# A fused attention and MLP block: a reciprocal root handed out in four pieces, weight loads moved behind transposes, the first V groups reordered, the last output columns narrowed

## The chip, the cores and the metric

The kernel runs on one core of one Trainium2 chip. The metric is the device time of one execution in microseconds (us), lower is better.

Terms: in the lines of the profile PE is the matmuls of TensorE, PEld its weight loads, DVE is VectorE, ACT ScalarE, POOL GpSimd, SPq the queue of SyncE; names such as r_a are buffers of the program. The granted clock is TensorE's clock as a share of its full speed. A drain is an instruction, here of DVE or ACT, that reads a finished accumulator, so that TensorE can use it again. A turn is a transpose. The root is the reciprocal root in a normalization.

## The reference

One transformer block in bf16: a pre-norm sliding-window attention with residual, then a pre-norm MLP with SiLU and residual. 2048 tokens, width 1024, 32 heads of 32, a window of 256 keys, hidden width 3584.

```python
x = A_x                                                     # [1, 2048, 1024]
h = x + A(_layernorm(x), A_wqkv, A_wo)                      # window attention, 32 heads x 32, W = 256
h2 = h + silu(_layernorm(h) @ B_w1) @ B_w2                  # 1024 -> 3584 -> 1024
return h2
```

## The kernel before

The tokens go in four blocks of 512. TensorE (matmul engine) is kept busy by interleaving: projections of block b with attention of block b-1, the output projection with attention of the last block, and at the end a dense stage without attention. In the dense stage each block has 28 groups of the first product (`h1_group`, 8 matmuls each) and then 8 output groups of the second product (28 matmuls each). Small work of other engines is kept in lists of steps, and the loops hand out one or two after each group.

The normalization of one block for the MLP (called LN2 here; LN1 is that before the attention) is such a list: a load of `h`, four statistics, one reciprocal root (12 tiny DVE operations), four normalizations, and four transposes by DMA. (The code here is cut at `...`, and some comments are added.)

```python
    def ln2_steps(b):
        ...
        steps = [load]
        steps += [lambda j=j: ln_stats(hb[:, j, :], st, j) for j in range(4)]
        steps.append(lambda: ln_rstd(st, rs, 0, 4))
        for j in range(4):
            steps.append(lambda j=j: ln_norm(hb[:, j, :], st, rs, j))
        turns = [lambda j=j: ln_transpose(hb[:, j, :], ln2T[b], j) for j in range(4)]
        return steps[:-2] + [turns[0], steps[-2], turns[1], steps[-1]] + turns[2:]
```

In the dense stage the LN2 steps of the *next* block are handed out, two after each of the eight output groups; what is left is issued after the last one. The next block's first product reads all four transposes (`rhs=ln2T[b][:, kt, :]` covers all 512 tokens).

```python
    for b in range(NB):
        ...
        for ft in range(FT):                       # 28 groups of the first product
            acc = h1_group(b, ft)
            run_late()                             # issues the transposes of attention
            if extra:                              # b == 0: rest of the last attention group
                extra.pop(0)[0]()
                if not extra and b == 0:
                    for i in (1, 2, 3, 4):
                        load_w2(i)                 # 1 MB each
            ...
        steps = ln2_steps(b + 1) if b + 1 < NB else []
        ...
        for j in range(4):
            ...
            for c in range(2):                     # 8 output groups
                ...                                # 28 matmuls, a DVE add, a store on the queue
                for _ in range(2):
                    if steps:
                        steps.pop(0)()
        while steps:
            steps.pop(0)()
```

All loads, stores and DMA transposes are issued from one queue (SyncE, "SPq" in the lines of the profile). The first V groups at the start of the kernel and the output projection (`wo_group`, which hands out LN2 of block 0 from its step n = 9 on) are in the whole kernel:

The softmax here doesn't subtract the row's maximum and nothing guards it: scores larger than these inputs give would overflow.

## Time and profile before

| | before |
|---|---|
| time, median of 3 runs | 709.64 us (708.79 to 709.89) |
| span of the profiled run, from first to last instruction | 708.9 us |
| TensorE busy | 695.2 us, 98% |
| longest waits of TensorE | 5.3, 1.6, 1.5 (in two), 1.3 us |
| first Q group starts (the V groups of the start end there) | 25.73 us |
| first dense matmul to first matmul of the second product (block 0) | 295.93 to 367.14 us |

The profiled run took 710.91 us, somewhat more than the median. TensorE is the bound; read its waits and the chain of waits, not the busy shares of the others. The lines are in the prediction.

### The profile page before, as it was taken

The page shows a single profiled execution, that of the slowest core. Times are in us where ns is not written, and L with a number is a line of the kernel's source. Part 1 is how long each engine was busy: PE and PEld are TensorE (multiplying, and loading weights), DVE is VectorE, ACT ScalarE, POOL GpSimd, SP SyncE. Part 2 cuts the span into 40 slices and gives each one's busy share as a digit, 9 for nine tenths or more (in the row PEclk, how much of TensorE's full clock was granted, in tenths as well). Part 3 has the DMA queues.
Part 4 walks back from the last instruction along what each step waited for, and adds up shares of the span by engine and source line. Part 5 has one row for each costly group of instructions (what it writes and reads, how often), then busy time and mean ns, then how long its engine had stood idle before and what let it go on. Part 6 is the DMA issues. An engine that isn't in the chain of part 4 may idle for free.

```text
span 708.9 us, 12138 instructions
## 1 busy us (share of the span) xinstructions
PE 695.2 (98%) x5006; PEld 332.8 (47%) x5006; DVE 288.0 (41%) x606; ACT 259.7 (37%) x335; POOL 172.9 (24%) x375
## 2 busy tenths in 40 slices
PE   8999999999999999979999999999999999999998
PEld 3444555555555554534444444444444444444443
DVE  5347645834443448523332423325134352243111
ACT  3416667777777777511220013300033200233000
POOL 1006566777777777500000000000000000000000
PEclk9999999999999999989999999999999999999999
DMA  9540322125011899780122320021410032200110
GB/s 301 173 120 8 46 54 75 32 55 180 16 23 18 279 265 333 201 276 31 45 69 90 80 75 1 0 67 59 78 35 0 1 97 67 75 1 0 31 38 22
DMA packets 75127, 60.55 MB, mean 85 GB/s; under 512 B 48960, under 2 KB 59200, under 8 KB 75072
## 3 DMA queue, kind: packets, MB, share of 16 engines
q1 hardware_dynamic: 75072, 59.78, 29.9%
q8 instruction: 39, 0.64, 0.4%
q14 instruction: 16, 0.13, 0.1%
HBM read 39.85 MB, written 8.39 MB: 68 GB/s over the span
## 4 chain that ended last, share of the span: by engine, by line
PE 94%; DMA 4%; DVE 2%; SPq 0%; issue 0%
PE hacc L446 18%; PE hacc L483 17%; PE acc L220 16%; PE acc L483 10%; PE acc L446 9%; PE acc L212 8%; PE acc L239 5%; PE o_ps L293 5%; PE sc L257 4%; DMA r_a<-r_n 2%; DMA r_w<-in_A_wqkv_dram 1%; PE hacc L239 1%; DMA r_a<-in_A_x_dram 1%; DVE ln_st L157 0%; DVE r_t L241 0%
## 5 line engine op out<-in xcount | busy, mean ns | idle before, releaser
L268 ACT ACTIVATE r_e<-sc 128x1024 bf16<-128x1024 f32 (+2 forms) x192 | 175.8, 967 | 67.5 <-PE sc L257 54.5
L283 POOL TENSOR_SCALAR_AFFINE_SELECT r_e<-r_e 128x256 bf16<-128x256 bf16 (+1 forms) x368 | 169.9, 490 | 123.1 <-ACT r_e L268 119.7
L446 PEld LDWEIGHTS <-r_w 128*128 128x128 bf16 x896 | 87.8, 98 | 106.1 <-issue 2.4
L483 PEld LDWEIGHTS <-r_a 128*128 128x128 bf16 x896 | 87.7, 98 | 105.7
L483 PE MATMUL hacc<-r_a 128*128 128x512 bf16 x560 | 122.3, 379 | 0.0
L446 PE MATMUL hacc<-r_e,r_w 128*128 128x512 bf16 x456 | 100.9, 379 | 0.0
L455 ACT ACTIVATE r_n<-hacc 128x512 f32<-128x512 f32 x30 | 17.9, 597 | 178.9 <-PE hacc L446 178.9
L483 PE MATMUL acc<-r_a 128*128 128x512 bf16 x336 | 74.0, 379 | 0.0
L220 PEld LDWEIGHTS <-r_w 128*128 128x128 bf16 x512 | 46.1, 98 | 58.6 <-issue 8.9
L222 DVE CAST r_a<-acc 128x512 bf16<-128x512 f32 x56 | 38.6, 690 | 81.0 <-PE acc L220 55.8
L293 PEld LDWEIGHTS <-r_e 128*128 128x128 bf16 x1440 | 50.3, 96 | 22.7
L220 PE MATMUL acc<-r_t,r_w 128*128 128x512 bf16 x256 | 60.8, 380 | 0.0
L220 PE MATMUL acc<-r_w 128*128 128x512 bf16 x256 | 58.2, 380 | 0.0
L293 PE MATMUL o_ps<-r_a,r_e 128*128 128x33 bf16 x1440 | 51.2, 178 | 0.0
L239 PE MATMUL acc<-r_o,r_a 128*128 128x512 bf16 x208 | 49.4, 380 | 1.3 <-DVE r_t L241 1.3
L446 PE MATMUL acc<-r_e,r_w 128*128 128x512 bf16 x216 | 49.1, 379 | 0.0
L239 PEld LDWEIGHTS <-r_a 128*128 128x128 bf16 x256 | 23.3, 98 | 37.2 <-issue 7.4
L257 PE MATMUL sc<-r_a 32*128 32x128 bf16 (+2 forms) x704 | 37.2, 276 | 0.0
L496 DVE SCALAR_TENSOR_TENSOR r_t<-hacc,r_t 128x512 bf16<-128x512 f32 x20 | 13.7, 683 | 56.3 <-PE hacc L483 56.2
L446 PE MATMUL hacc<-r_a,r_w 128*128 128x512 bf16 x144 | 34.6, 393 | 0.0
L496 DVE SCALAR_TENSOR_TENSOR r_t<-acc,r_t 128x512 bf16<-128x512 f32 x12 | 8.3, 692 | 64.2 <-PE acc L483 64.2
L456 DVE SCALAR_TENSOR_TENSOR r_a<-r_n,hacc 128x512 bf16<-128x512 f32 x30 | 20.6, 688 | 33.1 <-ACT r_n L455 33.1
(65 smaller groups left out, 425.4 us busy)
## 6 DMA issues: line engine op xcount, KB each, us to landing
r_w<-in_B_w_dram SPq DMA_DIRECT2D x8, 896.0 KB, 6.8
r_a<-in_B_w_dram SPq DMA_DIRECT2D x7, 1024.0 KB, 9.0
r_w<-in_A_wqkv_dram SPq DMA_DIRECT2D x5, 1024.0 KB, 11.8
r_o<-in_A_x_dram SPq DMA_DIRECT2D x16, 256.0 KB, 5.0
h_dram<-r_t SPq DMA_DIRECT2D x16, 256.0 KB, 2.9
r_t<-h_dram SPq DMA_DIRECT2D x16, 256.0 KB, 2.8
out_dram<-r_t SPq DMA_DIRECT2D x32, 128.0 KB, 1.7
r_e<-h_dram SPq DMA_DIRECT2D x3, 1024.0 KB, 5.8
```

What stands on the lines that cost most here:

```text
L212: nc.tensor.matmul(acc, lhsT=lnT_b[b % 2][:, kt, j * P:(j + 1) * P], rhs=wqkv[:, kt, col0:col0 + 512], start=(kt == 0), stop=(kt == KT - 1))
L220: nc.tensor.matmul(acc, lhsT=wqkv[:, kt, col0:col0 + P], rhs=lnT_b[b % 2][:, kt, :], start=(kt == 0), stop=(kt == KT - 1))
L222: copy(out=(qT, kT)[which][b][:, g, :], in_=acc)
L239: nc.tensor.matmul(acc, lhsT=qT[b][:, g, j * P:(j + 1) * P], rhs=wo[:, g, c * 512:(c + 1) * 512], start=(g == 0), stop=(g == G - 1))
L257: nc.tensor.matmul(sc[hh // 2][:, hh % 2, ch * P:(ch + nq) * P], lhsT=kT[t // 4][r0:r0 + DH, g, (t % 4) * P:(t % 4 + 1) * P], rhs=qT[b][r0 ...
L268: nc.scalar.activation(out=e[:, :, lo:hi], in_=sc[pair][:, :, lo:hi], func=ACT.Exp, scale=scale)
L283: nc.gpsimd.affine_select(out=ap, in_=ap, pattern=[[0, 2], [0, n], [sgn, P]], compare_op=ALU.is_ge if upper else ALU.is_gt, fill=0.0, base ...
L293: nc.tensor.matmul(o_ps[pair][:, qt * 2 + hh, 0:VW], lhsT=e_of(i, kind, pair)[:, hh, ch * P:(ch + 1) * P], rhs=v[:, b * 4 + kt, g * 4 + pa ...
L446: nc.tensor.matmul(acc, lhsT=w1[:, kt, ft * P:(ft + 1) * P], rhs=ln2T[b][:, kt, :], start=(kt == 0), stop=(kt == KT - 1))
L456: nc.vector.scalar_tensor_tensor(out=gT[:, ft, :], in0=th, scalar=1.0, in1=acc, op0=ALU.add, op1=ALU.mult)
L483: nc.tensor.matmul(acc, lhsT=gT[:, ft, j * P:(j + 1) * P], rhs=w2[ft // 4][:, ft % 4, c * 512:(c + 1) * 512], start=(ft == 0), stop=(ft == ...
L496: nc.vector.scalar_tensor_tensor(out=t_out[j % 2][:, c * 512:(c + 1) * 512], in0=acc, scalar=0.5, in1=t_in[j % 2][:, c * 512:(c + 1) * 512 ...
```

## The change

It has four intents: fill the waits for V weights at the start by another order of the V groups; keep DVE from standing in front of TensorE while it computes the root (the root becomes four steps: guess, and three Newton steps); let the last attention transposes go ahead of the w2 loads in the queue; and shorten the tail by narrow last output groups. The diff, cut to its core:

```diff
-    load_wqkv(2 * D, 0, 4)
+    load_wqkv(2 * D)
     load_x(0, 1)
-    load_wqkv(2 * D, 4, 8)
     load_wqkv(2 * D + 512)
...
-    for i in range(14):                              # warm-up matmuls
+    for i in range(11):
...
-    def ln_rstd(st, rs, lo, hi):
+    def rstd_steps(st, rs):
...                                                   # the same 12 operations
+        return [guess, newton, newton, newton]
...                                                   # V groups: (0,0) (0,1) (1,0) (1,1) ...
+    v_group(0, 0, 0, act)                            # now:      (0,0) (1,0) (0,1) (1,1) ...
+    turn_first(x_ring[1], lnT_b[0], 1)
+    ln_first(x_ring[2], st, rs, 2)
+    v_group(0, 1, 0, act)
+    v_group(0, 0, 1, act)
...
-        steps.append(lambda: ln_rstd(st, rs, 0, 4))  # in LN1 and in LN2 of every block
+        steps += rstd_steps(st, rs)
...
-            if n == 9:                               # output projection: LN2 of block 0
+            if n == 8:
                 steps = ln2_steps(0)
                 steps.pop(0)()
-            for _ in range(1 if n < 17 else 2):
-                if steps and n >= 12:
+            for _ in range(1 if n < 18 else 2):
+                if steps and n >= 10:
                     steps.pop(0)()
...
-                if not extra and b == 0:
-                    for i in (1, 2, 3, 4):
-                        load_w2(i)
+            if b == 0 and ft == 3:
+                for i in (1, 2, 3, 4):
+                    load_w2(i)
...
+            if b == NB - 1 and j == 3:
+                cols = [(0, 512), (512, 768), (768, 896), (896, 1024)]
```

More of the change, by code (lines that the diff above doesn't have):

```diff
@@ L126, in load_x, with load_wqkv @@
         nc.sync.dma_start(out=x_ring[(b % 2) * 4 + j], in_=x2d[(b * 4 + j) * P:(b * 4 + j + 1) * P, :])
-    def load_wqkv(c0, k0=0, k1=KT):
-        nc.sync.dma_start(out=wqkv[:, k0:k1, c0:c0 + 512], in_=wqkv_v[:, k0:k1, c0:c0 + 512])
+    def load_wqkv(c0):
+        nc.sync.dma_start(out=wqkv[:, :, c0:c0 + 512], in_=wqkv_v[:, :, c0:c0 + 512])
     load_x(0, 0)
-    load_wqkv(2 * D, 0, 4)
+    load_wqkv(2 * D)
     load_x(0, 1)
-    load_wqkv(2 * D, 4, 8)
     load_wqkv(2 * D + 512)
@@ L158, in ln_stats, with guess, newton @@
         nc.vector.bn_aggr(out=st[:, j, :], in_=stats[:])
-    def ln_rstd(st, rs, lo, hi):
-        n = hi - lo
+    def rstd_steps(st, rs):
         var = small.tile([P, 4], F32, name="ln_var", tag="ln_var")
         t = small.tile([P, 4], F32, name="ln_t", tag="ln_t")
-        va, ta, y = var[:, 0:n], t[:, 0:n], rs[:, lo:hi]
-        nc.vector.tensor_scalar(out=va, in0=st[:, lo:hi, 1], scalar1=LN_EPS, scalar2=None, op0=ALU.add)
-        nc.vector.tensor_scalar(out=y.bitcast(I32), in0=va.bitcast(I32), scalar1=1, scalar2=None, op0=ALU.logical_shift_right)
-        nc.vector.tensor_scalar(out=y.bitcast(I32), in0=y.bitcast(I32), scalar1=-1, scalar2=0x5F3759DF, op0=ALU.mult, op1=ALU.add)
-        for _ in range(3):
+        va, ta, y = var[:], t[:], rs[:]
+        def guess():
+            nc.vector.tensor_scalar(out=va, in0=st[:, :, 1], scalar1=LN_EPS, scalar2=None, op0=ALU.add)
+            nc.vector.tensor_scalar(out=y.bitcast(I32), in0=va.bitcast(I32), scalar1=1, scalar2=None, op0=ALU.logical_shift_right)
+            nc.vector.tensor_scalar(out=y.bitcast(I32), in0=y.bitcast(I32), scalar1=-1, scalar2=0x5F3759DF, op0=ALU.mult, op1=ALU.add)
+        def newton():
             nc.vector.scalar_tensor_tensor(out=ta, in0=y, scalar=-0.5, in1=va, op0=ALU.mult, op1=ALU.mult)
@@ L327 @@
     turn_first(x_ring[0], lnT_b[0], 0)
-    for j in range(4):
-        if j < 3:
-            ln_first(x_ring[j + 1], st, rs, j + 1)
-        v_group(0, j, 0, act)
-        if j < 3:
-            turn_first(x_ring[j + 1], lnT_b[0], j + 1)
-        v_group(0, j, 1, act)
-        if j == 2:
-            dummy = small.tile([P, 1], F32, name="dummy", tag="dummy")
-            nc.scalar.activation(out=dummy[:], in_=eps[:], func=ACT.Exp)
+    ln_first(x_ring[1], st, rs, 1)
+    v_group(0, 0, 0, act)
[3 more added lines that the diff above has]
+    v_group(0, 0, 1, act)
+    turn_first(x_ring[2], lnT_b[0], 2)
+    ln_first(x_ring[3], st, rs, 3)
+    v_group(0, 1, 1, act)
+    v_group(0, 2, 0, act)
+    turn_first(x_ring[3], lnT_b[0], 3)
+    v_group(0, 2, 1, act)
+    dummy = small.tile([P, 1], F32, name="dummy", tag="dummy")
+    nc.scalar.activation(out=dummy[:], in_=eps[:], func=ACT.Exp)
+    v_group(0, 3, 0, act)
+    v_group(0, 3, 1, act)
     for j in range(4):
@@ L355, in ln2_steps @@
         steps += [lambda j=j: ln_stats(hb[:, j, :], st, j) for j in range(4)]
-        steps.append(lambda: ln_rstd(st, rs, 0, 4))
+        steps += rstd_steps(st, rs)
         for j in range(4):
@@ L480, with mm2 @@
         steps = ln2_steps(b + 1) if b + 1 < NB else []
-        def mm2(acc, j, c, first, last):
+        def mm2(acc, j, c0, c1, first, last):
             for ft in range(first, last):
-                nc.tensor.matmul(acc, lhsT=gT[:, ft, j * P:(j + 1) * P], rhs=w2[ft // 4][:, ft % 4, c * 512:(c + 1) * 512],
+                nc.tensor.matmul(acc[:, 0:c1 - c0], lhsT=gT[:, ft, j * P:(j + 1) * P], rhs=w2[ft // 4][:, ft % 4, c0:c1],
                                  start=(ft == 0), stop=(ft == FT - 1))
@@ L488 @@
                 load_h(b, j + 1)
-            accs = [next_acc(), next_acc()]
-            if b == 0 and j == 0:
-                for c in range(2):
-                    mm2(accs[c], j, c, 0, FT - 4)
-            for c in range(2):
-                acc = accs[c]
-                mm2(acc, j, c, FT - 4 if b == 0 and j == 0 else 0, FT)
-                nc.vector.scalar_tensor_tensor(out=t_out[j % 2][:, c * 512:(c + 1) * 512], in0=acc, scalar=0.5,
-                                               in1=t_in[j % 2][:, c * 512:(c + 1) * 512], op0=ALU.mult, op1=ALU.add)
-                nc.sync.dma_start(out=out2d[(b * 4 + j) * P:(b * 4 + j + 1) * P, c * 512:(c + 1) * 512],
-                                  in_=t_out[j % 2][:, c * 512:(c + 1) * 512])
+            cols = [(0, 512), (512, 1024)]
+            if b == NB - 1 and j == 3:
+                cols = [(0, 512), (512, 768), (768, 896), (896, 1024)]
+            accs = [next_acc() for _ in cols]
+            early = FT - 4 if b == 0 and j == 0 else 0
+            for acc, (c0, c1) in zip(accs, cols):
+                mm2(acc, j, c0, c1, 0, early)
+            for acc, (c0, c1) in zip(accs, cols):
+                mm2(acc, j, c0, c1, early, FT)
+                nc.vector.scalar_tensor_tensor(out=t_out[j % 2][:, c0:c1], in0=acc[:, 0:c1 - c0], scalar=0.5,
+                                               in1=t_in[j % 2][:, c0:c1], op0=ALU.mult, op1=ALU.add)
+                nc.sync.dma_start(out=out2d[(b * 4 + j) * P:(b * 4 + j + 1) * P, c0:c1], in_=t_out[j % 2][:, c0:c1])
                 for _ in range(2):
```

## The prediction

> **What bounds the kernel now.** I read the page first, then the waits of TensorE, the chain that ended last, and the order of time on each engine around every gap of TensorE and around the places that the diff touches. TensorE is the bound: it is busy 98% of the span, and the chain runs through it from 12.46 us on. So a part of the change is worth what it does to TensorE's few gaps, and harms only if it makes a new one. The page's busy line, then the waits of TensorE (us in total, times, longest):
>
> ```profile
> PE 695.2 (98%) x5006; PEld 332.8 (47%) x5006; DVE 288.0 (41%) x606; ACT 259.7 (37%) x335; POOL 172.9 (24%) x375
> ...
> PE hacc L239 <- DMA r_a<-r_n: 5.3, 1, 5.3
> PE sc L151 <- DVE r_e L146: 1.6, 1, 1.6
> PE acc L212 <- DMA r_w<-in_A_wqkv_dram: 1.5, 2, 1.2
> PE acc L239 <- DVE r_t L241: 1.3, 1, 1.3
> ```
>
> The longest is one wait for a transpose by DMA of the last attention block (line 313, r_n to r_a). The chain of waits shows it with what follows (start us, us, what):
>
> ```profile
> 303.51 12.64 DMA r_a<-r_n
> 316.16 0.05 issue
> 316.20 0.61 PE hacc L239
> 316.81 3.41 PE hacc L446 x8
> 320.23 2.02 PE hacc L239 x8
> 322.25 1.73 PE hacc L446 x8
> ```
>
> The transpose took 12.64 us where the page has 2.5 us as its median: five w2 loads of 1 MB were issued from 297.98 us on, ahead of it in the same queue, and the DMA engines moved some 390 GB/s until 313. After the gap eight matmuls took 3.41 us where the same group later takes 1.73: the granted clock by single microseconds falls to 0.50 at 313.9 us and comes back at 320.7.
>
> The third place is the change of block in the dense stage, where the kernel before has no gap. In order of time (start us, us, engine, line, operation):
>
> ```profile
> 506.89 0.33 SPq L498 DMA_DIRECT2D out_dram<-r_t  x1
> 507.27 2.61 SPq L178 DMA_TRANSPOSE r_e<-r_e  x2
> 512.02 5.34 PE L446 MATMUL hacc<-r_e,r_w 128*128 128x512 bf16 x24
> 512.22 0.69 DVE L496 SCALAR_TENSOR_TENSOR r_t<-hacc,r_t 128x512 bf16<-128x512 f32 x1 [5.35 <-PE hacc L483]
> 512.94 0.33 SPq L498 DMA_DIRECT2D out_dram<-r_t  x1
> 513.31 0.93 SPq L225 DMA_DIRECT2D r_t<-h_dram  x2
> ```
>
> The last two transposes of the normalized block (line 178) are issued at 507.27, one output group ahead of the end of the block. The next block's first matmul (line 446), which reads all four, starts at 512.02 with no wait. The traffic in the windows of 1 us dies at 511.1, so the margin is under 1 us.
>
> **What the Trainium skill says.** "TensorE: Matmul & The Clock Gate", Part 1 (the HAM clock gate): the array runs at 1.2 GHz by default and 2.4 after a busy window of about 3.4 us, falls back after an idle one, and the windows run free. The trace agrees: clock down at 313.9, up at 320.7, which is two windows apart, and the first warm weight load at 6.65 us lies 90 windows before 313.9. "DMA: Bandwidth & Descriptors", Queues, rings and completion order: on each DMA engine descriptors are consumed in ring order. The 12.64 us transpose agrees. "Perfetto Trace Analysis", DMA Instruction, HWDGE: the slice of a DMA instruction ends when the sequencer is free, the movement of the data is not in it. The trace agrees: line 178 is 1.24 us on the queue, and 3.2 us from issue to landing by the page.
>
> **The change part by part.**
>
> 1. *w2 loads behind the transposes.* The loads of four of the five now follow the run of late issues, so the last transpose has only one 1 MB load ahead of it. It would be issued about when its data is there (303.2 in the old time) and land about 3 us later, at 306; its reader reaches it at 309 to 310.7. Hidden. Saved: without the gap the group from 309.22, one more and one more at 1.73 us each end at 314.4; they ended at 322.25. That is **-7.85 us** (5.3 gap, 2.5 slow clock). The w2 loads then end at about 317 (4 MB at 0.39 MB/us from 303 on, my estimate); their first reader starts at 367, so they stay hidden.
>
> 2. *Earlier load of the first block for LN2, steps spread (n = 8, 10, 18).* TensorE waited 1.3 us at 281.8 for a DVE that was late: DVE ran without pause from 267.4 to 283, and the whole root (12 tiny operations) sat between two drains of an accumulator, 277.81 to 282.50, 4.7 us. Spread over four cycles of 2.55 us, with the statistics starting a few us sooner, DVE keeps up by my walk through the cycles. Saved 1.3, less a little for turns that now end a cycle later, close before the first dense matmul: **-1.1 us**.
>
> 3. *Start.* The V groups swap just one pair: (1,0) now ahead of (0,1), to fill the 1.24 us wait for the second V weight at 12.46. But the first weight is now one 1 MB load ahead of x block 1. From the landings in the trace (x1 at 7.93 with 1 MB queued, the next half weight at 9.46 with 1.5 MB, the second weight at 12.46 with 2.5 MB: 0.5 MB per 1.5 us) x1 should land at 9.4 instead of 7.9, and from x1's landing to its V group took 3.7 us in like steps: 13.1. Then eight groups less one at 1.73 and two turns at 0.51 end at 26.25 where they ended at 25.73: **+0.5 us**. The other side is that the turn of block 2 was itself just in time (its x landed at 13.12), so the swap can gain next to nothing. The three warm-up matmuls dropped were over before anything that they delay mattered. I put +0.4.
>
> 4. *Narrow last output.* The last 512 columns (28 matmuls in 6.05 us) become 256, 128 and 128. Transposes of 128 columns took 0.51 us for eight, so 0.064 each; 28 twice are 3.6, and 256 columns at an estimated 0.115 are 3.2: TensorE +0.7. The last DVE add shrinks from 0.69 to about 0.3, the last store from 128 to 32 KB saves some 0.2 of its 1.7. Sum **+0.1 us**.
>
> 5. *Newton steps spread, where nobody had a problem.* This is the part that I think decides. In the dense stage each output group hands out two steps of the next block's normalization, eight groups, so sixteen. Before there were 14 steps (load, 4 statistics, 1 root, 4 normalizations, 4 transposes), so the last two transposes were handed out after the seventh group. Now there are 17. The eighth group gets the fourth normalization and the third transpose, and the fourth transpose is left over. The order of instructions of the changed kernel confirms it: on the DMA queue both come behind the store of the eighth group, on DVE the last normalization behind the eighth add. The eighth add needs the end of the block on TensorE, and the next block's first matmul needs the transposes. So TensorE stands. From the rows above: TensorE ends at 512.0, add and store of the eighth group let the queue go at 513.31 (1.2 to 1.3 us after the end), two transposes from issue to quiet DMA were 507.27 to 511.1, with the semaphore about 4.0. Gap: 1.2 + 4.0 + 0.1 = **5.3 us**. The normalization (0.54 after the add) is done before the second is issued. A gap of 5.3 us also loses the clock, just as the same 5.3 us did at 311: there it cost 2.5 us. With windows of 3.41 us at a random phase I get 1.2 to 3.1, mean 2.1; I take 2.2. Per change of block 7.5, and there are three: **+22.5 us**.
>
> Sum: 709.6 - 7.85 - 1.1 + 0.4 + 0.1 + 22.5 = 723.6. I give 723.4, since the clock may be kept once.
>
> **The rivals.**
> - *The turns of the dense stage are hidden anyway.* Then only parts 1 to 4 count: about 701 us, 1.2% faster. For it speaks that this is what the change is meant for; against it the order on both queues and the margin under 1 us already. I give it 5%.
> - *The gap is there but the clock is kept,* because no window falls wholly into it: 3 x 5.3 = 16, hence 717. Against it: the gap at 311 lost the clock with 15% of its window still busy. 8%.
> - *The gap is there and the clock comes back late* (3.1 us each), or the start also runs cold, since x1's late landing leaves TensorE idle for 1.7 and 1.5 us around 7 and 11 us: 726 to 728. 10%.
> - *DVE waits in the LN2 stage for the block loaded too early,* and blocks a drain: statistics now stand in its queue at 262, and the load lands at perhaps 262.6 to 265. It would give back up to 1 us of part 2.
>
> **Range and chances.** The gap is uncertain by 0.3 us, three times alike: 0.9. The clock's phase: 0.6 each, 1.0 for three. Start 0.6, the rest 0.5. Together 1.6, or 2.1 to either side for 8 in 10; the rivals widen it below. Range 719.8 to 726.2. The 2% line is 723.8, almost on the prediction, so the two outcomes are near even: slower by over 2% 0.42, within 2% 0.55, faster 0.03.
>
> **What would show it.** In the profile after: three waits of TensorE at line 455, for a transpose r_e to r_e, 5 to 5.6 us each, at about 408, 512 and 616 us, each followed by 3 to 6 us at a granted clock of 0.5; no wait for r_a from r_n, and that transpose under 5 us; the wait for DVE in the output projection gone or under 0.5; the first Q group starting near 26 us; three small DVE adds at the end. I am wrong if the waits at line 455 are missing or under 3 us, or if the start loses or gains over 1.5 us.

## The result, and the profile after

| | before | after |
|---|---|---|
| time in the same rounds, median | 709.24 us (708.79 to 709.89) | **726.06 us** (725.14 to 727.75) |
| span of the profiled run | 708.9 us | 723.5 us |
| mean granted clock of TensorE | 0.995 | 0.988 |

All outputs are right. The ratio is 1.0239, 95% interval 1.0215 to 1.0264: slower by 2.4%. Ratios here are the mean time of one kernel's runs over that of the other's in the same rounds, so not quite the ratio of the medians quoted.

Cut at four marks in both traces, the spans differ like this:

| stretch of TensorE's chain | before | after | difference |
|---|---|---|---|
| start of the span to first Q group | 25.73 | 24.11 | -1.6 |
| to the first dense matmul | 270.20 | 270.35 | +0.15 |
| to the first matmul of the second product | 71.21 | 63.53 | -7.7 |
| from there to the end | 341.76 | 365.51 | **+23.75** |

So the change earned 9 us in two stretches, nothing in one, and lost 24 in the last. Now to the lines. The page's busy line and granted clock, kernel after (the clock is in tenths, in 40 slices of the span):

```profile
PE 693.8 (96%) x4970; PEld 336.4 (46%) x5059; DVE 286.0 (40%) x608; ACT 259.9 (36%) x335; POOL 171.4 (24%) x375
...
PEclk9999999999999999999999999999899999899999
```

The busy time of TensorE is hardly changed (693.8 against 695.2), while its share fell from 98 to 96%: the time went into waits, and two 8s show in the clock. The waits of TensorE, kernel after (us in total, times, longest):

```profile
PE hacc L455 <- issue: 11.5, 2, 5.8
PE hacc L455 <- DMA r_e<-r_e: 5.7, 1, 5.7
PE acc L242 <- DVE r_t L244: 1.9, 1, 1.9
```

Line 455 is the first product. It waits three times, 17.2 us in all, 5.7 to 5.8 each. For one the profile names the transpose; the two "issue" are waits whose releaser it did not match, and the order of time shows the same there. The second change of block, kernel after, in order of time (start us, us, engine, line, operation; in brackets the idle time before and its releaser). Line 177 normalizes, 181 transposes, 507 is the output add, 509 the store:

```profile
505.42 1.23 SPq L181 DMA_TRANSPOSE r_e<-r_e  x1
510.37 0.69 DVE L507 SCALAR_TENSOR_TENSOR r_t<-hacc,r_t 128x512 bf16<-128x512 f32 x1 [4.90 <-PE hacc L492]
510.98 0.54 DVE L177 TENSOR_SCALAR r_e<-r_e,st_b,rs_b 128x1024 bf16<-128x1024 bf16 x1
511.09 0.33 SPq L509 DMA_DIRECT2D out_dram<-r_t  x1
511.46 2.60 SPq L181 DMA_TRANSPOSE r_e<-r_e  x2
...
516.05 7.66 PE L455 MATMUL hacc<-r_e,r_w 128*128 128x512 bf16 x24 [5.72 <-issue]
```

Before, the pair of transposes came ahead of the end of the block and its reader never waited. After, the pair is issued at 511.46, behind the add and the store of the eighth group. TensorE had ended at 516.05 - 5.72 = 510.33, so the queue was free 1.13 us later, and from issue to the reader's start it took 4.59 (4.58 and 4.61 at the two other changes of block). Then 24 matmuls took 7.66 us where the same 24 took 5.34 in the kernel before. The windows of 1 us say why, kernel after (busy PE, PEld, DVE, ACT, POOL, then the granted clock, the DMA share and GB/s):

```profile
513.00:514.00 1.00, 0.00 (x0) 0.00 (x0) 0.00 (x0) 0.00 (x0) 0.00 (x0) 0.97 1.03 194
514.00:515.00 1.00, 0.00 (x0) 0.00 (x0) 0.00 (x0) 0.00 (x0) 0.00 (x0) 0.50 1.02 198
...
520.00:521.00 1.00, 1.00 (x5) 0.34 (x3) 0.69 (x1) 0.25 (x1) 0.00 (x0) 0.61 0.00 0
521.00:522.00 1.00, 1.00 (x6) 0.44 (x5) 0.00 (x0) 0.00 (x0) 0.00 (x0) 1.00 0.00 0
```

The clock falls to a half inside the gap and is back only at 520.8, almost 5 us after work resumed. The 24 matmuls behind the three gaps took 6.75, 7.66 and 8.09 us, against 5.34 in the kernel before. So the clock cost 1.41, 2.32 and 2.75 us, 6.5 together. A wait is counted from the end of the last matmul, 0.38 us after its start, while without a wait the next one starts 0.22 after it (512 columns at the full clock: 28 in 6.04). That is 0.16 more per gap, so the gaps cost 17.7 and not 17.2. Gaps 17.7 and clock 6.5 make 24.2; the end gave back 0.4. That is the +23.75.

Where the gain came from: the chain of waits around the old 5.3 us gap, kernel after (start us, us, what), and the queue there:

```profile
307.92 1.73 PE hacc L242 x8
309.65 1.73 PE hacc L455 x8
311.37 1.73 PE hacc L242 x8
```

```profile
301.79 1.19 SPq L316 DMA_TRANSPOSE r_a<-r_n  x1
303.03 2.51 SPq L446 DMA_DIRECT2D r_a<-in_B_w_dram  x4
```

The transpose is issued ahead of the four loads, no gap is left, and the group takes 1.73 us, not 3.41. The second product starts without a wait at 357.99, so the later loads are hidden.

### The profile page after: what moved, and what is told of

Its sections match the earlier page's. It is cut to its first block, busy times and chain, and to the rows that moved or that the text cites. A ratio compares the mean times of both kernels' runs of the same rounds, so it can differ in the third digit from the quotient of the medians.

```text
span 723.5 us, 12167 instructions
## 1 busy us (share of the span) xinstructions
PE 693.8 (96%) x4970; PEld 336.4 (46%) x5059; DVE 286.0 (40%) x608; ACT 259.9 (36%) x335; POOL 171.4 (24%) x375
## 4 chain that ended last, share of the span: by engine, by line
PE 93%; DMA 3%; issue 1%; DVE 1%; SPq 1%; POOL 0%; ACT 0%; POOLq 0%; ACTq 0%
PE hacc L455 19%; PE hacc L492 17%; PE acc L223 16%; PE acc L492 10%; PE acc L455 9%; PE acc L215 8%; PE acc L242 5%; PE o_ps L296 5%; PE sc L260 4%; PE hacc L242 1%; DMA r_e<-r_e 1%; DMA r_o<-in_A_x_dram 1%; DMA r_w<-in_B_w_dram 1%; POOL r_e L286 0%; DVE ln_st L156 0%
## 5 line engine op out<-in xcount | busy, mean ns | idle before, releaser
L492 PEld LDWEIGHTS <-r_a 128*128 128x128 bf16 x952 | 90.9, 98 | 103.0
L455 PE MATMUL hacc<-r_e,r_w 128*128 128x512 bf16 x444 | 106.7, 397 | 17.8 <-issue 11.5
L492 PE MATMUL hacc<-r_a 128*128 128x512 bf16 (+2 forms) x605 | 121.9, 359 | 0.6
L242 PEld LDWEIGHTS <-r_a 128*128 128x128 bf16 x256 | 23.2, 98 | 31.5 <-issue 6.9
L507 DVE SCALAR_TENSOR_TENSOR r_t<-hacc,r_t 128x512 bf16<-128x512 f32 (+2 forms) x22 | 13.9, 633 | 59.1 <-PE hacc L492 59.1
L455 PE MATMUL hacc<-r_a,r_w 128*128 128x512 bf16 x141 | 32.7, 379 | 0.2
```

What stands on the lines that cost most here:

```text
L242: nc.tensor.matmul(acc, lhsT=qT[b][:, g, j * P:(j + 1) * P], rhs=wo[:, g, c * 512:(c + 1) * 512], start=(g == 0), stop=(g == G - 1))
L455: nc.tensor.matmul(acc, lhsT=w1[:, kt, ft * P:(ft + 1) * P], rhs=ln2T[b][:, kt, :], start=(kt == 0), stop=(kt == KT - 1))
L492: nc.tensor.matmul(acc[:, 0:c1 - c0], lhsT=gT[:, ft, j * P:(j + 1) * P], rhs=w2[ft // 4][:, ft % 4, c0:c1], start=(ft == 0), stop=(ft == F ...
L507: nc.vector.scalar_tensor_tensor(out=t_out[j % 2][:, c0:c1], in0=acc[:, 0:c1 - c0], scalar=0.5, in1=t_in[j % 2][:, c0:c1], op0=ALU.mult, o ...
```

## The experiments

All runs were beside runs of the kernel before on the same chip: its medians were 708.88 and 708.76 in the first two series, 708.99 in the last. The kernel after itself did not run again in them, so a difference from its 726.06 us is one of medians of different series.

### The root as one step again, in the kernel after

```diff
-        steps += rstd_steps(st, rs)
+        root = rstd_steps(st, rs)
+        steps += root if b == 0 else [lambda: [f() for f in root]]
```

> The changed kernel, but the root of blocks 1 to 3 is one step again (14 steps for eight output groups). My theory, that the loss is the last two transposes handed out behind the eighth group: no wait of TensorE at the change of block, span 723.5 - 24.2 = 699.3, time 700 to 702 us, faster than before by 1.2 to 1.4%. Rival, that the transposes are late for another reason of the change (a fuller DMA queue, the other issue order): gaps of 3 us or more stay, time over 710.

Measured: 700.62 us (699.75 to 701.34), ratio to before 0.9883 [0.9869, 0.9898]. Its span is 697.7 us, and the waits of TensorE that are left are those of the start:

```profile
PE sc L150 <- DVE r_e L145: 1.6, 1, 1.6
PE acc L215 <- ACT r_w L195: 0.6, 2, 0.4
PE o_ps L194 <- DVE r_o L177: 0.5, 1, 0.5
```

So all of the loss hangs on the number of steps: 25.4 us by the medians, 25.8 by the spans, of which 1.9 is the wait for DVE in the output projection, which does not belong to it and comes and goes (below). The other 23.9 agree with the 24.2 read from the gaps. The same 12 operations are executed in the same order.

### The split root kept, three steps handed out while more than eight are left

```diff
-                for _ in range(2):
+                for _ in range(3 if len(steps) > 8 else 2):
```

> The changed kernel with all 17 steps, but three of them handed out after each of the first three groups, so that the transposes fall where they did before. Theory: it is the place of the transposes, not the spreading of the root: time within 0.5 us of the kernel with the whole root, 700 to 702 us. Rival, that the spread root itself is slower on DVE or that three steps at once hold up a drain: 2 us or more over that kernel.

Measured: 700.38 us (700.01 to 701.24), 0.9882 [0.9867, 0.9897]. This undoes nothing of the split; it only brings the 17 steps into the first seven groups (three times three, four times two). The same place in order of time, this kernel:

```profile
496.38 0.33 SPq L509 DMA_DIRECT2D out_dram<-r_t  x1
496.76 2.86 SPq L181 DMA_TRANSPOSE r_e<-r_e  x2
```

This is the store of the seventh group, with the pair of transposes behind it, and TensorE starts the next block at 501.51 with no wait. The margin is small: here, as in the kernel before, 4.75 us lie between the issue and the reader, and 4.6 were needed in the kernel after. Splitting the root is harmless; handing it out too slowly is not.

### Useless matmuls in the gap

The 24 matmuls of 512 columns, some 5.2 us of work at the full clock, are put into the queue of TensorE after blocks 0 to 2. They read w1 and write a bank that nobody reads; the result stays correct.

```diff
+        if b + 1 < NB:
+            for i in range(24):
+                nc.tensor.matmul(o_ps[0].rearrange("p a b -> p (a b)"), lhsT=w1[:, 0, 0:P], rhs=w1[:, 0, 0:512], start=True, stop=True)
```

> The changed kernel with 24 matmuls of no use (into a bank that is free by then) behind each of the first three blocks, which fill some 5.2 us of the gap of 5.7. It does not shorten the gap. Theory, that 7.0 us of the 24.2 are the clock: granted clock stays 1.0 at the changes of block, the first 24 matmuls after take 5.2 us each time, time 726 - 7 = 719 us (718 to 720). Rival, that the slow matmuls after the gap come from their weights or from the DMA traffic then: time stays at 725 to 728.

Measured: 717.79 us (717.42 to 719.44), 1.0131 [1.0115, 1.0146], span 715.9; the median is 0.2 under the range expected. The waits of TensorE at the change of block, this kernel:

```profile
PE hacc L455 <- issue: 1.6, 3, 0.6
```

The wait for the transposes is as long as it was, 5.2 us of it now filled and about 0.5 left, but the clock stayed at 1.00. The span fell by 7.6 against the kernel after. Of that, 1.5 is a shorter wait in the output projection (0.4, not 1.9), and the start took 0.4 more; what remains, about 6.5, is the clock, as the lengths of the matmuls say (the 7.0 of the expectation counted the 0.16 per gap to it). So the loss has two parts of about 17.7 and 6.5, and the second can be had back without touching the wait.

### Each part alone, in the kernel before

The spread of the root in blocks 1 to 3 only:

```diff
-        steps.append(lambda: ln_rstd(st, rs, 0, 4))
+        if b == 0:
+            steps.append(lambda: ln_rstd(st, rs, 0, 4))
+        else:
+            steps += rstd_steps(st, rs)
```

> The kernel before with only the root of blocks 1 to 3 spread over four steps. Theory: all the loss and nothing else: three gaps of 5.7 us, 16 to 19 us of gap and 5 to 9 of slow clock, time 709.2 + 24 = 731 to 735 us. Rival, that the loss needs the other parts too: under 720.

Measured: 734.48 us (733.95 to 735.66), 1.0367 [1.0349, 1.0384]. The waits of TensorE, this kernel, where line 466 is the first product and the third line is the old gap, untouched:

```profile
PE hacc L466 <- issue: 11.7, 2, 5.8
PE hacc L466 <- DMA r_e<-r_e: 5.9, 1, 5.9
PE hacc L256 <- DMA r_a<-r_n: 5.4, 1, 5.4
```

It costs 25.6 us by the medians; taken out of the kernel after it gave 25.4. The two directions agree.

The w2 loads only:

```diff
-                if not extra and b == 0:
-                    for i in (1, 2, 3, 4):
-                        load_w2(i)
+            if b == 0 and ft == 3:
+                for i in (1, 2, 3, 4):
+                    load_w2(i)
```

> The kernel before with only four w2 loads moved behind the last attention transpose. Theory: the wait of 5.3 us for r_a from r_n and the slow clock after it go, and nothing comes in their place: 7.7 us less (71.2 to 63.5 us from the first dense matmul to the first of the second product, as in the changed kernel), time 700.7 to 702.0 us. Rival, that part of the gain comes from the spread root and the earlier load: 5 us less or fewer.

Measured: 701.56 us (700.48 to 703.94), 0.99 [0.9873, 0.9926]. From the first dense matmul to the second product it took 295.01 to 358.54, that is 63.53 us, the same as in the kernel after and 7.7 less than before. No wait for r_a from r_n is left.

The first V weight in one load of 1 MB, nothing else:

```diff
-    load_wqkv(2 * D, 0, 4)
+    load_wqkv(2 * D)
     load_x(0, 1)
-    load_wqkv(2 * D, 4, 8)
     load_wqkv(2 * D + 512)
```

> The kernel before with only the first V weight in one load of 1 MB instead of two of 0.5 with x block 1 between. The recorded prediction has x block 1 landing later and the first Q group 0.5 us later (26.2). After the result I think the opposite: x block 2 lands near 11.0 as in the changed kernel, the first Q group starts at 24.1 to 24.6 instead of 25.7, time 1 us less. Rival, since the kernel before has shown 24.7 too, under the same start, in the run with the spread root only: the landings vary from run to run, and the time is within 0.5 us of before.

Measured: 708.15 us (706.71 to 710.23), 0.999 [0.9973, 1.0008]: by the time, nothing is resolved, and the 1 us that was expected is not seen. In the profile the first Q group's matmuls start at 23.55 us and not at 25.57, as far ahead as in the kernel after (23.94). (These are starts of matmuls, 0.16 before the marks 25.73 and 24.11 of the chain.)

The new order of the V groups, nothing else (the diff is that of the change):

> The kernel before with only the new order of the V groups. Prediction: no gain, since the turn of block 2 is just in time either way: within 0.4 us of before, first Q group 24.6 to 25.8. Rival, that the order makes the start of the changed kernel quicker: 0.8 us or more less, first Q group at 24.2.

Measured: 708.65 us (708.43 to 710.52), 1.0001 [0.9988, 1.0014]. The first Q group's matmuls start at 24.80, which lies within the scatter of the other kernels with two half loads (24.51, 25.57, 25.66). No gain of the order is to be seen.

The profiles of the two runs say that the start gained by the single load and not by the order; their times are too close to say it. The statistics of the third token tile wait for its x. Kernel before, then kernel after:

```profile
13.12 1.29 DVE L157 BATCH_NORM_STATS2 ln_st<-r_o 128x6 f32<-128x512 bf16 x2 [2.35 <-DMA r_o<-in_A_x_dram]
```

```profile
11.00 1.29 DVE L156 BATCH_NORM_STATS2 ln_st<-r_o 128x6 f32<-128x512 bf16 x2 [0.85 <-DMA r_o<-in_A_x_dram]
```

In the four profiles with two half loads these statistics start at 12.07 to 13.22 us, in the ten with one load at 11.00 to 11.47. The transfers go with it: between 5 and 6 us the former move 189 to 221 GB/s, the latter 339 to 369. Kernel before, then kernel after (columns as above):

```profile
5.00:6.00 1.00, 1.00 (x4) 0.39 (x3) 0.60 (x3) 0.29 (x1) 0.00 (x0) 1.00 0.78 216
```

```profile
5.00:6.00 1.00, 0.96 (x4) 0.19 (x2) 0.60 (x3) 0.29 (x1) 0.00 (x0) 1.00 1.06 357
```

The first Q group's matmuls start at 24.5 to 25.7 in the four and at 23.6 to 24.4 in the ten, on average 1.1 us earlier: part of the 1.6 between the two kernels compared above is scatter. Why a 256 KB load between two half loads lets the rate sink there stays open.

### A version with all gains, and the order of LN2

The last doubt was the wait of 1.9 us for DVE in the output projection, where the change was meant to save 1.3. This kernel is the one with three steps, with the statistics of block 0 handed out from n = 11 and not from 10:

```diff
-            for _ in range(1 if n < 18 else 2):
-                if steps and n >= 10:
+            for _ in range(1 if n < 17 else 2):
+                if steps and n >= 11:
```

> The changed kernel with three steps after each of the first three groups, and in the output projection the statistics from cycle 11 and two steps from 17 instead of 10 and 18. Theory: in the profiled run of the changed kernel DVE stood 4.3 us at the first statistics for the block's load, and TensorE waited 1.9 us for a drain behind it; with one cycle more the drain goes first, so no wait there: 0 to 0.3 us. But two runs of the same order showed no such wait, so the time is within 0.7 us of the kernel it is made from (700.4). Rival: the wait is in most runs, and the time falls by 1 us or more, to 699.

Measured: 699.52 us (699.43 to 699.61), 0.9868 [0.9852, 0.9885], no wait for DVE; 0.9 under the kernel it is made from, between what theory and rival had. In the last series it and its base ran again, unchanged:

> The same with the statistics from cycle 11, once more, on the same chip as its base. Theory, that it takes the wait for DVE out of all runs: 0.5 to 1.2 us under its base and single runs within 0.5 us of each other. Rival, that the first comparison was of two chips: within 0.3 us of the base.

> The changed kernel with three steps after each of the first three groups once more, as the base for the three beside it, on the same chip: 700.0 to 701.2 us, with single runs over 1 us apart, since the wait for DVE in the output projection comes in some runs and not in others.

Measured: 699.49 us (699.38 to 701.85), 0.9871 [0.9851, 0.9892], against 701.05 us (699.58 to 701.49), 0.9883 [0.9864, 0.9903], for the base. The times overlap, so a difference is not resolved by them, and against the expectation the single runs with n = 11 were not within 0.5 us of each other in this series. The profiles tell it: with statistics from n = 11 four profiles of four show no wait for DVE; from n = 10 the five profiles (the kernel after, and the experiments on it) show 1.9, 0, 0, 0.4 and 1.8 us, where the second 0 and the 1.8 are the same kernel, the base, run twice. DVE's order of time in the second run of the base has the cause:

```profile
264.58 1.29 DVE L156 BATCH_NORM_STATS2 ln_st<-r_a 128x6 f32<-128x512 bf16 x2 [4.16 <-DMA r_a<-h_dram]
```

The statistics stand at the head of DVE's queue for 4.16 us, for a block load that has not landed, and the drain of TensorE's accumulator stands behind them. That is the prediction's fourth rival, and it happened. The wait of 1.3 us in the kernel before was no fixed amount either: the five profiles with the old hand-out (the kernel before, and the experiments on it) show 1.3, 0.7 and 0.4, 0.4, none and 0.4 us. Whether the spread of the root takes any of it away was not tested apart from the order.

The old order of the V groups, one load kept, in this best kernel (the diff of the change at that place, backwards):

> The kernel with the statistics from cycle 11, and the V groups in their old order; the one load stays. In the run with one load only, group (0,1) started right behind the turn at 10.45, where in the changed kernel group (1,0) waited for ScalarE's copy until 10.95. Theory: the new order costs 0.3 to 0.5 us, first Q group at 23.5 instead of 24.0, time 0.3 to 0.6 us less. Rival, the intent of the change: the old order is slower, by 0.5 us or more, since the second V weight comes later than the first.

Measured: 699.52 us (699.07 to 700.09), 0.9866 [0.9845, 0.9887]; the first Q group starts at 23.67 and not at 23.97. The new order gains nothing here either, and the 0.3 us or more that the old one was to save are not in the time. In the profiles with one load the new order is the later one: 23.55 and 23.67 with the old order, 23.94 to 24.37 in the eight with the new.

The last output 512 wide again, in the best kernel:

```diff
-            if b == NB - 1 and j == 3:
-                cols = [(0, 512), (512, 768), (768, 896), (896, 1024)]
```

> The kernel with the statistics from cycle 11, and the last output 512 columns wide again. Prediction on record: the narrow last output costs 0.1 us, so this is 0.1 us faster. Rival, from the changed kernel's profile (8.92 us from the start of the last 512 columns to the end against 9.34): 0.4 us slower.

Measured: 699.84 us (699.45 to 701.76), 0.9874 [0.9852, 0.9897]. The times do not resolve it. In the profiles, from the start of the add before the last columns to the end of the span it takes 698.2 - 688.84 = 9.36 us wide, 697.4 - 688.51 = 8.89 narrow: the narrow end is worth about 0.45 us. The last add, kernel after:

```profile
720.76 0.29 DVE L507 SCALAR_TENSOR_TENSOR r_t<-hacc,r_t 128x128 bf16<-128x128 f32 x1 [1.27 <-PE hacc L492]
```

## Why the prediction was right, and where it was not

It was right: 726.06 us lies in its range of 719.8 to 726.2, but 0.1 us from the edge and 2.7 above the 723.4 that it gave. "Slower by over 2%" came out, to which it gave 0.42; it had put 0.55 on "within 2%". One of its own signs of being wrong came true: the start gained 1.6 us between the two profiles, where the sign was over 1.5.

| step of the prediction | predicted | measured in the traces |
|---|---|---|
| 1. w2 loads | -7.85 | -7.7 |
| 2. LN2 in the output projection | -1.1 | +0.15 |
| 3. start | +0.4 | -1.6 |
| 4. narrow end | +0.1 | -0.4 |
| 5. three changes of block | +22.5 | +24.2 |
| sum | +14.1 | +14.6 |

**Step 5, the mechanism.** Shown by three runs. Fewer steps (the whole root) and faster handing out both take the whole loss away, and the split alone, put into the kernel before, makes it. The first rival, that these turns are hidden anyway, predicted about 701 us and is refuted.

**Step 5, the size.** The gap was 5.7 us, not 5.3. The term that was too small is the 4.0 us from the issue of two transposes to the reader: it was taken from the moment that the traffic died in the kernel before, and it measured 4.6. The prediction had better numbers at hand: the second transpose goes out 1.3 us after the first, and the page's 3.2 us from issue to landing make that 4.5. The time to free the queue was right (1.13 against 1.2). The clock cost 6.5 us where 3 x 2.2 = 6.6 was put, with the three values between 1.41 and 2.75, inside the stated 1.2 to 3.1. The rival that keeps the clock is refuted by the kernel after itself, and filling the gap shows that the clock is a separate part.

**Step 1** was right in mechanism and size; the run of it alone measured 63.53 us in that stretch too.

**Step 2 failed.** It credited the spread with -1.1. The kernel after waits for DVE 1.9 us, the kernel before 1.3, and the wait varies from profile to profile with both hand-outs, so that 1.3 was never a sure gain. In the kernel after the wait is not the root's: it comes from where the statistics stand in DVE's queue against the landing of the block load; the rival named that, with up to 1 us, and it should have been weighed more.

**Step 3 failed in sign.** It took the landings to follow the bytes queued ahead, 0.5 MB per 1.5 us, and put x of the second tile at 9.4 us. Its statistics started at 7.32 us. The rate that this law was read from came from the kernel with two half loads, and the single load alone already moves it. The 1.6 us is of one pair of profiles; over all of them the gain is about 1.1. It was right that the order gains next to nothing.

**Step 4** took 0.064 us for a matmul of 128 columns from a row of transposes; 28 took 1.56, that is 0.056. TensorE's extra time was 0.13 (3.05 for 256 columns and twice 1.56, against 6.04) and not 0.7, and the sign turned.

The five steps err by +0.15, +1.25, -2.0, -0.5 and +1.7. They cancel to about +0.5, so that the sum of spans is better than its terms: that is luck. Against the medians, +16.8 us, the sum is 2.7 short. Beside the 0.5, that comes from the choice of runs: the profiled run of before was 1.7 slower than its median of 709.24, and the one of after 0.9 faster than its 726.06 (and time less span is 0.3 smaller in the latter).

The kernel that keeps the change's gains and hands the steps out in time runs in 699.5 us, 1.3% faster than before and, by medians of different series, 3.7% faster than the change.

## What to carry to other kernels

When a step that a fixed-rate loop hands out is split, count the steps against the slots up to the consumer: here three more steps on sixteen slots moved two transposes behind the last store and cost 24 us, although no work was added. In an in-order queue the urgent item's place counts more than its length, for the DMA queue (a transpose of 2.5 us by the median took 12.6 behind 5 MB) as for DVE (statistics waiting for a load ahead of a drain). A gap of TensorE can cost the clock as well: here each of 5.7 us cost 1.4 to 2.8 us on top, and matmuls of no use in the gap kept the clock.

## What the Trainium skill lacked or had wrong

- "TensorE: Matmul & The Clock Gate", Part 1 speaks of an idle and of a busy window without saying how idle or busy. By window arithmetic on the traces (an estimate): the clock fell after a window 13% busy (kernel before, at 313.9 us; the prediction says 15), windows 38 and 64% busy did not bring it back (second and third gap of the kernel after), and one 85% busy did (first gap). The kernel with the spread alone narrows it: in its second gap TensorE began again at 525.27 in a window from 524.28 to 527.69, 71% busy, and the clock stayed low; in the third it began at 630.87 in one from 630.10 to 633.51, 77% busy, and the clock came back. So in these traces the border to come back lies between 71 and 77%.
- The same page, "Back-to-back issue gap", has about 131 ns for a sustained 512-column matmul and 81 for 128 columns, each with its weight load, and says that the isolated formula misjudges both. Here, each with a new weight load, 512 columns took 216 ns (28 in 6.04 us) and 128 columns 56 ns (28 in 1.56 us): the formula's figures hold.
- "DMA: Bandwidth & Descriptors", Latency and other measured facts, has a rate for DMA transposes, and "VectorE: DVE Perf Modes" a duration for one of 128x128, but neither has a time from issue to reader. Here two of 128x1024 in bf16 took 4.6 us from the issue of the first to the reader's start in the kernel after (4.7 in the one with the spread alone).
- No page has the dip at the start: two loads of 0.5 MB with one of 256 KB between them moved 189 to 221 GB/s between 5 and 6 us and the tile after them was used at 12.07 to 13.22 us, against 339 to 369 GB/s and 11.00 to 11.47 with one load of 1 MB. The cause is open.
